# Attention taken two slots at a time in the mixed loop of an attention and mixture-of-experts kernel

## The chip, the cores and the metric

The kernel runs as one program on one core of a Trainium2 chip. The metric is the device time of one execution in microseconds (us); the time before is the median of three runs. The engines are named as in the profile: PE (TensorE, with PEld for its weight loads), DVE (VectorE), ACT (ScalarE), POOL (GpSimd) and SP (SyncE, which here only issues DMAs).

## The reference

Three layers follow each other. The second and the third are dense in everything but the choice of one expert per token.

```
# attention: 4 batches x 8 heads, 512 local and 32 global tokens, head dimension 64
out_g = softmax(q_g @ [k_g, k_l].T / 8) @ [v_g, v_l]                # global rows see all
s_l   = [q_l @ k_g.T, where(|i - j| <= 32, q_l @ k_l.T, -1e9)] / 8   # local rows: band of 65, and the globals
out_l = softmax(s_l) @ [v_g, v_l]
x = concat(out_g, out_l) as (2176, 512)
# dense layer, 512 -> 2048 -> 512
h = x @ w_in;  x = max(0.01 h, h) @ w_out
# routed layer, 8 experts, 512 -> 1024 -> 512
e = argmax(normalised x @ normalised expert_emb.T / tau)
out = gate * (relu(x @ w1[e]) @ w2[e])
```

## The kernel before

**Slots of attention.** The local attention is cut into 64 slots, two for each pair of 128-row chunks of a pair of heads; `m = n // 4` is the pair of heads of slot `n`. `att_parts(n)` lists what slot `n` issues:

- an even slot: `AV(p)` for `p = (n - 4) / 2` (lines 355 and 361, probabilities times values into `av`, copied to `xr`); then `softmax(n // 2)`, which is `S` (line 248, 32 small matmuls into the two score tiles `sp`), `M` (line 276, four masked row maxima on DVE; line 284, four exponentials on ACT) and `N` (lines 297 to 304, the division);
- every slot: `TR(n - 2)` (line 319, three transposes of probabilities into `pp`, copied to `pT` by ACT);
- a slot with `n % 4 == 1`: the keys of the next pair of heads, `kp` (line 217, copied to `kT` by ACT) and `gnp` (line 223, copied by DVE, line 225); with `n % 4 == 3`: the queries, `qp` (line 200, copied to `qz` by ACT);
- for the global rows, once in eight slots: `GS` (lines 388 and 389, scores into `sg1` and `sg2`; maxima on DVE, lines 392 to 394; exponentials into `pg` on ACT, lines 398 and 399) at slot 36 and at slots 43, 51 and 59; `GT` (lines 413 and 415, transposes `gp` and `gq`) at slots with `n % 8 == 6`; `GA4` in two pieces, `ga` (line 455) at `n % 8 == 7` and `gb` (line 460) at the next slot.

Slots 0 to 35 run in a front part with an order of its own, which the change does not touch. Slots 36 to 67 run in the mixed loop.

**The mixed loop.** It goes over `steps`, pairs `(i, f)` of the dense layer: 256 tokens `i` by 128 columns `f` of the hidden layer. A step issues `L1(i, f)` (line 850, 12 matmuls into `hps`), then perhaps a slot of attention, then `L2` of the step before (lines 877 to 879, 6 matmuls into `yp`), then perhaps one stage of the routing of finished tokens: `R1` (line 625, `x2p`), `R2` (line 636, `lp`), `R3` (lines 655 and 656, `rp`). Between `L1` and its `L2` stands a chain of four instructions: ACT `gf` (line 858), DVE maximum (line 860), ACT cast (line 863), DVE remainder (line 865). After the last step of a token block `R0` copies `yp` on ACT (line 614) and squares it (line 617).

A credit grows by 0.65 or 0.6 with each step. A slot is taken when it reaches 1:

```
credit += RATE[min(i, len(RATE) - 1)]
...
if credit >= 1.0 and slot < bound:
    run(att_parts(slot))
    slot += 1
    credit -= 1.0
credit = min(credit, 1.0)
```

**What sets the order.** PE runs in the order in which the program is written. DVE, ACT, POOL and SP are ordered when the program is built, by priorities (`ahead` raises that of most attention parts); once built, each engine runs its own list from first to last.

**PSUM.** The eight banks are four tags of two buffers each: `H` for `hps`, `Y` for `yp`, and in the loop `S` for `av`, one half of `sp`, `pp` and `sg1`, and `T` for everything else: the other half of `sp`, `sg2`, `kp`, `qp`, `gnp`, `gp`, `gq`, `ga`, `gb`, `x2p`, `lp`, `rp`. A matmul into a tag waits until the last reader of the buffer that it gets is done.

Of the kernel before, what the change touches and what calls it, by code (L numbers as in the profile page):

```python
# [24 lines left out]
def kernel(  # L25
# [22 lines left out]
    E, _, F2 = w1.shape  # L48
# [34 lines left out]
    def whole(job):  # L83
        for _ in job:
            pass
# [14 lines left out]
    def load_k(n):  # L100
        b, h0 = n // HP, 2 * (n % HP)
        if n % 2 == 0:
            yield SP, 2.0, "kn gn", "", 1.6
        else:
            yield SP, 1.0, "kn", "", 1.3
        kn = att.tile([P, NC, 2, D], F32, tag="kn", bufs=2, name="kn")
        rows(n, kn, k_l)
        if n % 2 == 0:
            gn = att.tile([2 * SG, 4 * D], F32, tag="gn", bufs=2, name="gn")
            for i, src in enumerate((q_g, k_g)):  # L110
                nc.sync.dma_start(
                    gn[i * SG:(i + 1) * SG].rearrange("s (h d) -> s h d", h=4),
                    src[b, h0:h0 + 4].rearrange("h s d -> s h d"),
                )
        else:
            gn = natural["gn"]
        natural["gn"] = gn
        natural["k", n] = kn, gn[:, (n % 2) * 2 * D:(n % 2 + 1) * 2 * D]

    def load_q(n):  # L120
        yield SP, 1.0, "qn", "", 1.3
        qn = natural["q", n] = att.tile([P, NC, 2, D], F32, tag="qn", bufs=1, name="qn")
        rows(n, qn, q_l)
# [254 lines left out]
    def GS(n):  # L378
        a1, a2 = bank_of("sg1"), bank_of("sg2")
        yield PE, 1.08, f"{a1} {a2}", kt_tag(n)  # L380
        sg1 = ps.tile([P, SL - SG], F32, tag=a1, name="sg1")
        sg2 = ps.tile([P, 2 * SG], F32, tag=a2, name="sg2")
        for j in range(4):
            o = slice(SG * j, SG * j + SG)
            kT, qg = qkT[n - 1 + j // 2]
            r = slice(D * (j % 2), D * (j % 2) + D)
            at = (D * (j % 2), SG * j)
            nc.tensor.matmul(sg1[o, :], qg[r], kT[r, 2 * SG:S_], start=True, stop=True, tile_position=at)  # L388
            nc.tensor.matmul(sg2[o, :], qg[r], kT[r, 0:2 * SG], start=True, stop=True, tile_position=at)
        yield DVE, 1.07, "", ""  # L390
        gm = att.tile([P, 4], F32, tag="gm", bufs=2, name="gm")
        nc.vector.tensor_reduce(out=gm[:, 0:1], in_=sg1, axis=AX.X, op=ALU.max, negate=True)
        nc.vector.tensor_reduce(out=gm[:, 1:2], in_=sg2, axis=AX.X, op=ALU.max, negate=True)
        nc.vector.tensor_scalar(
            out=gm[:, 0:1], in0=gm[:, 0:1], scalar1=gm[:, 1:2], scalar2=0.125, op0=ALU.min, op1=ALU.mult
        )
        yield ACT, 1.3, "pg", f"{a1} {a2}"
        nc.scalar.activation(out=pg[:, 0:SL - SG], in_=sg1, func=AF.Exp, bias=gm[:, 0:1], scale=0.125, accum_out=gm[:, 2:3])  # L398
        nc.scalar.activation(out=pg[:, SL:], in_=sg2, func=AF.Exp, bias=gm[:, 0:1], scale=0.125, accum_out=gm[:, 3:4])
        yield DVE, 0.37, "", ""  # L400
        nc.vector.tensor_scalar(
            out=gm[:, 2:3], in0=gm[:, 2:3], scalar1=gm[:, 3:4], scalar2=1e-9, op0=ALU.add, op1=ALU.add
        )
        nc.vector.reciprocal(out=gm[:, 2:3], in_=gm[:, 2:3])
        yield POOLL, 1.1, "", ""
        nc.gpsimd.tensor_tensor(out=pg, in0=pg, in1=gm[:, 2:3].to_broadcast([P, SL + 2 * SG]), op=ALU.mult)

    def GT(n):
        a1, a2 = bank_of("gp"), bank_of("gq")
        yield PE, 0.6, f"{a1} {a2}", "pg"  # L410
        gp = ps.tile([P, NC, P], F32, tag=a1, name="gp")
        for c in range(NC):
            nc.tensor.transpose(gp[:, c, :], pg[:, c * P:(c + 1) * P], ident)
        gq = ps.tile([2 * SG, P], F32, tag=a2, name="gq")
        nc.tensor.transpose(gq, pg[:, SL:], ident)
        yield DVE, 0.27, "gu", a2
        gu = att.tile([2 * SG, P], F32, tag="gu", bufs=1, name="gu")
        nc.vector.tensor_copy(gu, gq)
        by = yield (ACT, DVE), (0.59, 0.67), "PT", a1
        gt = att.tile([P, NC, P], F32, tag="PT", bufs=2, name="gt")  # L420
        copy(by, gt, gp)
        groups[n] = gt, gu
# [473 lines left out]
    late = {}  # L896
# [433 lines left out]
    LAG, AVL = 2, 4  # L1330

    def ahead(by, f, *a):
        with tc.high_priority(offset=by):
            whole(f(*a))

    def att_parts(n):

        parts = []
        m = n // 4
        p = (n - AVL) // 2  # L1340
        if n % 2 == 0 and 0 <= n - AVL < NU:
            if p in sums:
                parts.append(lambda: ahead(0, BR, p))
            parts.append(lambda: ahead(0, AV, p))
        early = m % 2 == 1 and n % 4 == 2 and m < NHP
        if early:
            parts.append(lambda: whole(GT(m)))
        if n < NU and n % 2 == 0 and not early:
            parts.append(lambda: ahead(50, softmax, n // 2))
        if m % 2 == 1 and n % 4 == 3 and m < NHP:  # L1350
            late["ga"] = GA4(m)
            parts.append(lambda: next(late["ga"]))
        if 0 <= n - LAG < NU:
            parts.append(lambda: ahead(50, TR, n - LAG))
        if early:
            parts.append(lambda: ahead(50, softmax, n // 2))
        if n % 4 in (1, 3) and m + 1 < NHP:
            parts.append(lambda: ahead(50, QK, m + 1, n % 4 // 2))
        if n % 8 == 0 and "ga" in late:
            parts.append(lambda: whole(late.pop("ga")))  # L1360
        if n == SLOT0 or n > SLOT0 and n % 8 == 3 and m + 1 < NHP:
            parts.append(lambda: whole(GS((n + 4) // 8 * 2 + 1 if n > SLOT0 else m)))
        if n % 4 == 3:
            if m + 3 < NHP:
                parts.append(lambda: whole(load_k(m + 3)))
            if m + 2 < NHP:
                parts.append(lambda: whole(load_q(m + 2)))
        for v in range(2, NHP):
            if n == 4 * (v - 2) + max(AVL + 2, 7 - v % 2):
                parts.append(lambda v=v: whole(load_v(v)))  # L1370
        return parts


# [23 lines left out]
    def run(parts):  # L1397
        for p in parts:
            p()
# [3 lines left out]
    SLOT0 = 36  # L1403
# [11 lines left out]
        BR=[-72.8, 427.3, 393.7, 659.9, 354.6, 181.8, 728.1, 127.1, 127.4, 513.3, 141.3, 12.2, 477.9, 672.5, 305.3,  # L1415
            338.0, 255.6],
# [7 lines left out]
        GS=[0.0, -360.1, 0.0, 390.9, 0.0, 458.7, 0.0, 442.6],  # L1424
        AV=[-608.9, -583.3, -939.5, -865.4, -876.7, -658.5, 89.6, -629.4, -191.7, -506.2, 13.6, -135.5, -415.6,
            414.4, -43.5, 327.5],
        GT=[0.0, -1032.9, 0.0, -450.7, 0.0, -353.5, 0.0, -170.3],
# [207 lines left out]
    while k < len(steps):  # L1635
        i, f = steps[k]
        store_rows()
        if k == KF * (2 * B - 1) + 6:
            assert not pend_r
            plan_constants()  # L1640
            early_plan()
            load_w(0, zip(lane, (w1, w2)))
            to_split(0, lane, False)
            for u in range(NEARLY):
                load_ids(u)
            for u in range(2):
                gather(u)
        if k == K0 + 1:
            routing_rows()
            fetch_part()  # L1650
        credit += RATE[min(i, len(RATE) - 1)]
        bound = min(LAST, AVL + 16 * (2 + i // 2) + (2 if i % 2 == 1 and i > 1 else 0))
        bank = MIXED
        mp = moe_parts(i, f)
        run(mp[:1])
        if credit >= 1.0 and slot < bound:
            run(att_parts(slot))
            slot += 1
            credit -= 1.0
        credit = min(credit, 1.0)  # L1660
        run(mp[1:])
        if pend_r:
            st, t = pend_r.pop(0)
            st(t)
        if k >= KF * (2 * B - 1) + 10:
            for _ in range((2, 1, 1, 2, 1, 1)[k - KF * (2 * B - 1) - 10]):
                tc.keep_in_program_order(piece())
        if slot == LAST and att is not None:
            att_pool.__exit__(None, None, None)
            att = None  # L1670
            lp_ = late["pool"] = ctx.enter_context(tc.tile_pool(name="lane", bufs=1))
            lane += [lp_.tile([P, KM, F2], F32, name="w1a"), lp_.tile([P, KF2, DM], F32, name="w2a")]
        k += 1
# [205 lines left out]
```

## Time and profile before

| | |
|---|---|
| three runs, median (lowest to highest) | 817.11 us (816.13 to 820.07) |
| the profiled execution | 820.54 us, of which the profile's span is 818.8 us |
| PE busy | 795.5 us, 97% of the span |
| PEld, DVE, ACT, POOL busy | 661.5, 401.7, 371.7, 200.0 us |
| slots 36 to 67 of the mixed loop | from 199.6 to 420.4 us of the span |
| granted clock of PE, mean | 0.995 of 2.4 GHz |

The profile's PE share counts a matmul as busy until its modelled end, so that a busy PE may still be waiting for the next weights. The times of the section on the rows are microseconds from the start of the span.

### The profile page before, as it was taken

To read this page: it belongs to the slowest core of one execution; us is meant where nothing else is said; L and a number is where in the kernel's file an instruction comes from. 1 tells how busy PE (TensorE), PEld (TensorE's weight loads), DVE (VectorE), ACT (ScalarE), POOL (GpSimd) and SP (SyncE) were. 2 spreads that over 40 slices of the span, in tenths; PEclk is the share of its full clock that TensorE was granted. 3 is DMA by queue.
4 is the path that set the end of the run, shared out by engine and by line. 5 is a ranking of instruction groups with operands and counts; after the bars stand their busy time and mean duration, and the time that the engine had idled before them with its cause. 6 is when DMAs were issued, how large, how long until landed. Compare 5 with 4: busy or idle time off the path is not lost.

```text
span 818.8 us, 17489 instructions
## 1 busy us (share of the span) xinstructions
PE 795.5 (97%) x6818; PEld 661.5 (81%) x6818; DVE 401.7 (49%) x1200; ACT 371.7 (45%) x1006; POOL 200.0 (24%) x294
## 2 busy tenths in 40 slices
PE   7989999999999999999999999999999999989996
PEld 5778878888888888888888888898899886858642
DVE  4788775635645554554552533546453525215230
ACT  5776676545534544544532323335323425224441
POOL 4767986801110010000010100002101421111100
PEclk9999999999999999999999999999999999999998
DMA  8967585610122220211000000071049796997890
GB/s 196 233 156 188 159 207 156 198 40 18 46 60 45 65 49 21 42 37 17 2 27 1 14 14 1 27 206 52 26 46 227 234 398 251 358 391 253 333 368 25
DMA packets 111885, 106.18 MB, mean 130 GB/s; under 512 B 75879, under 2 KB 84199, under 8 KB 111794
## 3 DMA queue, kind: packets, MB, share of 16 engines
q1 hardware_dynamic: 107314, 95.53, 39.5%
q0 software_dynamic: 3424, 9.20, 3.4%
q8 instruction: 55, 0.90, 0.5%
q14 instruction: 36, 0.29, 0.2%
q10 hardware_dynamic: 1056, 0.26, 0.1%
HBM read 94.13 MB, written 11.10 MB: 129 GB/s over the span
## 4 chain that ended last, share of the span: by engine, by line
PE 79%; DMA 8%; issue 7%; DVE 3%; ACT 1%; SPq 1%; POOL 1%; POOLq 0%; ACTq 0%
PE hps L850 24%; PE yp L877 8%; PE yp L879 7%; PE yp L878 7%; PE hps L1297 6%; PE yp L1315 6%; DMA out_dram<-yo,ids 4%; PE sp L248 3%; PE pp L319 3%; PE av L355 2%; DMA wm<-in_moe_w_dram 2%; PE av L361 2%; PE lp L636 1%; PE sg L388 1%; PE sc L334 1%
## 5 line engine op out<-in xcount | busy, mean ns | idle before, releaser
L858 ACT ACTIVATE gf<-hps 128x256 f32<-128x256 f32 (+1 forms) x144 | 53.7, 373 | 155.1 <-PE hps L850 143.4
L860 DVE TENSOR_TENSOR hps<-hps,gf 128x256 f32<-128x256 f32 (+1 forms) x144 | 59.9, 416 | 110.9 <-ACT gf L858 109.8
L877 PE MATMUL yp<-woh,g 128*128 128x512 f32 x272 | 111.5, 410 | 0.8 <-ACT g L863 0.8
L879 PE MATMUL yp<-woh,g 128*128 128x512 f32 x272 | 107.5, 395 | 0.0
L878 PE MATMUL yp<-wol,g 128*128 128x512 f32 x272 | 107.4, 395 | 0.0
L865 DVE TENSOR_TENSOR g<-hps,g 128x256 fp32r<-128x256 f32 (+1 forms) x144 | 58.4, 406 | 44.1 <-ACT g L863 43.5
L863 ACT CAST g<-hps 128x256 fp32r<-128x256 f32 (+1 forms) x144 | 52.1, 362 | 56.6 <-DVE hps L860 47.1
L850 PE MATMUL hps<-xs,wih 128*128 128x256 f32 x448 | 75.6, 291 | 0.5 <-ACT pg L398 0.4
L1315 PE MATMUL yp<-w2s,g 128*128 128x512 f32 x288 | 75.5, 395 | 0.0
L850 PE MATMUL hps<-xl,wih 128*128 128x256 f32 x448 | 70.7, 279 | 0.0
L850 PE MATMUL hps<-xs,wil 128*128 128x256 f32 x448 | 70.7, 279 | 0.0
L850 PEld LDWEIGHTS hps<-xs,wih 128*128 128x128 f32 x448 | 64.0, 188 | 7.0 <-issue 0.7
L1297 PE MATMUL hps<-xgT,w1s 128*128 128x256 f32 x384 | 61.9, 283 | 0.4 <-ACT xgT L1192 0.4
L879 PEld LDWEIGHTS yp<-woh,g 128*128 128x128 f32 x272 | 51.0, 188 | 12.6 <-DVE g L865 0.2
L850 PEld LDWEIGHTS hps<-xs,wil 128*128 128x128 f32 x448 | 60.5, 188 | 0.0
L850 PEld LDWEIGHTS hps<-xl,wih 128*128 128x128 f32 x448 | 60.5, 188 | 0.0
L877 PEld LDWEIGHTS yp<-woh,g 128*128 128x128 f32 x272 | 51.0, 188 | 9.9 <-ACT g L863 1.4
L1315 PEld LDWEIGHTS yp<-w2s,g 128*128 128x128 f32 x288 | 50.8, 187 | 10.0 <-issue 0.8
L1297 PEld LDWEIGHTS hps<-xgT,w1s 128*128 128x128 f32 x384 | 54.0, 188 | 3.7 <-ACT xgT L1192 0.7
L878 PEld LDWEIGHTS yp<-wol,g 128*128 128x128 f32 x272 | 51.2, 188 | 6.7
L1303 ACT ACTIVATE g<-hps 128x256 fp32r<-128x256 f32 x48 | 18.5, 385 | 77.3 <-PE hps L1297 72.1
L1304 DVE SCALAR_TENSOR_TENSOR g<-hps,g 128x256 fp32r<-128x256 f32 x48 | 20.4, 424 | 64.6 <-ACT g L1303 60.3
(314 smaller groups left out, 1517.0 us busy)
## 6 DMA issues: line engine op xcount, KB each, us to landing
wm<-in_moe_w_dram SPq DMA_DIRECT2D x14, 2048.0 KB
w1a<-in_moe_w_dram SPq DMA_DIRECT2D x6, 2048.0 KB
w2a<-in_moe_w_dram SPq DMA_DIRECT2D x6, 2048.0 KB
raw<-in_moe_w_in_dram SPq DMA_DIRECT2D x16, 512.0 KB
raw<-in_moe_w_out_dram SPq DMA_DIRECT2D x16, 512.0 KB
x2d<-x SPq DMA_DIRECT2D x16, 256.5 KB
kn<-in_k_l_dram SPq DMA_DIRECT2D x31, 128.0 KB
qn<-in_q_l_dram SPq DMA_DIRECT2D x31, 128.0 KB
```

Source lines behind the costliest of these rows:

```text
L248: nc.tensor.matmul(sps[h][HALF_ * half:HALF_ * half + HALF_, to:to + width], qz[r, t:t + HALF_], kT[r, from_:from_ + width], start=not fro ...
L319: nc.tensor.transpose(pp[:, j, :], pr[:, from_:from_ + P], ident)
L850: nc.tensor.matmul(hps, ws[a][:, k], xs[c][k], start=(a + c + k == 0), stop=((a, c) == (1, 0) and k == KM - 1))
L858: nc.scalar.activation(out=gf, in_=hps[:, cs], func=AF.Copy, scale=0.01)
L860: nc.vector.tensor_tensor(out=hps[:, cs], in0=hps[:, cs], in1=gf, op=ALU.max)
L863: nc.scalar.copy(g[:, 0], hps[:, cs])
L865: nc.vector.tensor_tensor(out=g[:, 1], in0=hps[:, cs], in1=g[:, 0].bitcast(F32), op=ALU.subtract)
L877: nc.tensor.matmul(yp, g[:, 0], hi, start=begins(i, f), stop=False)
L878: nc.tensor.matmul(yp, g[:, 0], lo, start=False, stop=False)
L879: nc.tensor.matmul(yp, g[:, 1], hi, start=False, stop=ends(i, f))
L1297: nc.tensor.matmul(hps, w[:, a, k, fs], xts[u][c][:, k], start=(a + c + k == 0), stop=(a == 1 and k == KM - 1))
L1315: nc.tensor.matmul(ys[u, t], g[:, a, t * P:(t + 1) * P], w[:, c, f % 4, :], start=(f + a + c == 0), stop=(f == KF2 - 1 and a == 1),)
```

## The change

Two slots are taken in one step, when the credit reaches 2, and the credit is capped at 2. Their parts are issued one slot behind the other, each slot in its old order. Each part now carries a number in front, which nothing in the loop reads.

```
-                parts.append(lambda: ahead(0, BR, p))
-            parts.append(lambda: ahead(0, AV, p))
+                parts.append((0, lambda: ahead(0, BR, p)))
+            parts.append((0, lambda: ahead(0, AV, p)))
...
-            parts.append(lambda: ahead(50, TR, n - LAG))
+            parts.append((3 + 4 * (n % 2), lambda: ahead(50, TR, n - LAG)))
...
-        if credit >= 1.0 and slot < bound:
-            run(att_parts(slot))
-            slot += 1
-            credit -= 1.0
-        credit = min(credit, 1.0)
+        if credit >= 2.0 and slot < bound:
+            parts = att_parts(slot) + att_parts(slot + 1)
+            run([fn for _, fn in parts])
+            slot += 2
+            credit -= 2.0
+        credit = min(credit, 2.0)
```

The 32 slots of the loop become 16 pairs, (36, 37) to (66, 67). Worked from the rates, they fall in steps 32, 35, 38, 41, 45, 48, 51, 55, 58, 64, 67, 70, 73, 77, 80 and 83 of the loop. Before, the even slots stood in steps 32, 35, 38, 42, 45, 48, 52, 55, 58, 64, 67, 70, 74, 77, 80 and 84, and each odd slot one to three steps behind its even one.

PE around slots 36 and 37, before. `sg` are the two tiles of `GS`, `kp` and `gnp` the keys of the next pair of heads.

```order
L389 MATMUL sg_3184<-kT 32x64
L877 MATMUL yp<-woh,g 128x512 [waits Activation_49]
L878 MATMUL yp<-wol,g 128x512
...
L636 MATMUL lp<-enT,x2T 128x8 [waits DVE_49,PE_49]
...
L850 MATMUL hps<-xs,wil 128x256 x4
L319 MATMUL pp<-ident,pr_105 128x128 [waits Activation_49]
...
L217 MATMUL kp<-ident,kn 128x128 [waits DMAHW2_49,DMAHW1_49,Activation_49]
...
L223 MATMUL gnp<-ident,gn 128x64 [waits DMAHW4_49,DMAHW3_49,DVE_49]
```

The same place after:

```order
L389 MATMUL sg_3184<-kT 32x64
L319 MATMUL pp<-ident,pr_105 128x128 [waits Activation_49]
...
L217 MATMUL kp<-ident,kn 128x128 [waits DMAHW2_49,DMAHW1_49,DVE_49]
...
L223 MATMUL gnp<-ident,gn 128x64 [waits DMAHW4_49,DMAHW3_49,Activation_49]
L877 MATMUL yp<-woh,g 128x512
L878 MATMUL yp<-wol,g 128x512
```

`L2`, a routing stage and the next `L1` no longer stand between `sg` and `gnp`, and `gnp` now waits for ACT.

ACT at this place, before (`pg` are the exponentials of `GS`, `sq` the squares of `R0`):

```order
L284 ACTIVATE pr_104,sm<-pr_104,nm 128x160 [waits DVE_49] x3
L398 ACTIVATE pg,gm<-sg_3183,gm 128x480 [waits DVE_49,PE_49]
L399 ACTIVATE pg,gm<-sg_3184,gm 128x64 [waits PE_49]
L617 ACTIVATE sq,ss<-x_2935 128x512 [waits PE_49]
...
L858 ACTIVATE gf<-hps 128x256 [waits PE_49]
L81 COPY pT<-pp 128x384 [waits PE_49]
L649 ACTIVATE lg,ss<-lg,ss 128x8 [waits DVE_49]
L81 COPY kT<-kp 128x512 [waits PE_49]
```

And after:

```order
L284 ACTIVATE pr_104,sm<-pr_104,nm 128x160 [waits DVE_49] x3
L81 COPY pT<-pp 128x384 [waits PE_49]
L81 COPY kT<-kp 128x512 [waits PE_49,Pool_49]
L398 ACTIVATE pg,gm<-sg_3183,gm 128x480 [waits DVE_49]
L399 ACTIVATE pg,gm<-sg_3184,gm 128x64
L617 ACTIVATE sq,ss<-x_2935 128x512 [waits DVE_49,PE_49]
```

The copies of slot 37 now stand ahead of the exponentials of slot 36.

PE at slots 42 and 43 after. Before, an `L2` and an `L1` stood between the two `pp`, which belong to one slot each:

```order
L319 MATMUL pp<-ident,pr_104 128x128 [waits DVE_49]
...
L319 MATMUL pp<-ident,pr_104 128x128 [waits DVE_49,PE_49]
...
L200 MATMUL qp<-ident,qn 128x128 [waits DMAHW5_49,DMAHW4_49]
...
L388 MATMUL sg_3828<-kT 32x480 [waits Activation_49]
L389 MATMUL sg_3829<-kT 32x64 [waits DVE_49]
```

The second `pp` stands right behind the first and waits for DVE.

## Rows read from the trace of the kernel before

**Rows 1.** Windows, PE: stretch, length, busy (instructions), granted clock, DMA share, GB/s.

```profile
196.00:424.00 228.00, 227.15 (x2332) 1.00 0.16 36
```

**Rows 2.** Waits of PE between 196 and 425 us: total, times, longest.

```profile
PE x2p L625 <- ACT x L614: 0.6, 2, 0.3
PE sg L388 <- DVE nm L276: 0.3, 1, 0.3
```

**Rows 3.** Chain of waits at slots 36 and 37: start, time it took, what.

```profile
200.70 0.87 PE sp L248 x32
...
202.28 1.02 PE sg L388 x8
...
203.43 0.43 PE yp L877
...
207.33 0.33 PE pp L319 x3
207.66 0.44 PE kp L217 x4
...
209.93 1.52 PE hps L850 x12
211.45 0.23 PE yp L877
```

**Rows 4.** Chain of waits at slots 38 to 40.

```profile
215.28 0.46 PE av L355 x16
...
218.12 0.43 PE yp L877
...
222.01 0.83 PE ga L455 x40
222.84 0.48 PE pp L319 x3
...
229.93 0.61 PE av L355 x16
...
232.26 0.11 PE gb L460
232.37 0.24 PE yp L877
```

**Rows 5.** Timeline of DVE at slots 36 and 40: start, busy, instruction [idle before it].

```profile
201.56 0.32 DVE L276 CUSTOM_DVE_ANT_0 pr<-sp,mask 128x160 f32<-128x160 f32 x1
...
202.29 0.32 DVE L276 CUSTOM_DVE_ANT_0 pr<-sp,mask 128x160 f32<-128x160 f32 x1
...
203.51 0.66 DVE L392 TENSOR_REDUCE gm<-sg 128x1 f32<-128x480 f32 x1 [0.89 <-PE sg L389]
...
232.82 0.44 DVE L462 COPY xgl<-gb 64x64 f32<-64x64 f32 x2
```

**Rows 6.** Timeline of ACT at slots 36 and 37.

```profile
202.35 0.46 ACT L81 COPY pT<-pp 128x384 f32<-128x384 f32 x1
...
203.86 0.19 ACT L284 ACTIVATION_READ_ACCUMULATOR pr<-pr,nm 128x1 f32 x1
205.27 0.66 ACT L398 ACTIVATE pg<-sg,gm 128x480 f32<-128x480 f32 x1 [1.21 <-DVE sm L300]
...
205.92 0.31 ACT L399 ACTIVATE pg<-sg,gm 128x64 f32<-128x64 f32 x1
...
208.55 0.58 ACT L81 COPY kT<-kp 128x512 f32<-128x512 f32 x1
```

**Rows 7.** Chain of waits at slot 46, where a token block ends.

```profile
274.92 0.48 ACT x L614
```

**Rows 8.** Windows of PE in the front part and near the end, columns as in rows 1.

```profile
59.00:60.00 1.00, 0.60 (x12) 0.78 0.05 10
...
62.00:63.00 1.00, 1.00 (x20) 0.51 1.28 316
...
710.00:720.00 10.00, 7.30 (x51) 1.00 1.04 392
```

More of the change, by code (lines that the diff above doesn't have):

```diff
@@ L1342, in att_parts @@
             if p in sums:
-                parts.append(lambda: ahead(0, BR, p))
-            parts.append(lambda: ahead(0, AV, p))
+                parts.append((0, lambda: ahead(0, BR, p)))
+            parts.append((0, lambda: ahead(0, AV, p)))
         early = m % 2 == 1 and n % 4 == 2 and m < NHP
         if early:
-            parts.append(lambda: whole(GT(m)))
+            parts.append((1, lambda: whole(GT(m))))
         if n < NU and n % 2 == 0 and not early:
-            parts.append(lambda: ahead(50, softmax, n // 2))
+            parts.append((2, lambda: ahead(50, softmax, n // 2)))
         if m % 2 == 1 and n % 4 == 3 and m < NHP:
             late["ga"] = GA4(m)
-            parts.append(lambda: next(late["ga"]))
+            parts.append((5, lambda: next(late["ga"])))
         if 0 <= n - LAG < NU:
-            parts.append(lambda: ahead(50, TR, n - LAG))
+            parts.append((3 + 4 * (n % 2), lambda: ahead(50, TR, n - LAG)))
         if early:
-            parts.append(lambda: ahead(50, softmax, n // 2))
+            parts.append((4, lambda: ahead(50, softmax, n // 2)))
         if n % 4 in (1, 3) and m + 1 < NHP:
-            parts.append(lambda: ahead(50, QK, m + 1, n % 4 // 2))
+            parts.append((6, lambda: ahead(50, QK, m + 1, n % 4 // 2)))
         if n % 8 == 0 and "ga" in late:
-            parts.append(lambda: whole(late.pop("ga")))
+            parts.append((8, lambda: whole(late.pop("ga"))))
         if n == SLOT0 or n > SLOT0 and n % 8 == 3 and m + 1 < NHP:
-            parts.append(lambda: whole(GS((n + 4) // 8 * 2 + 1 if n > SLOT0 else m)))
+            parts.append((9, lambda: whole(GS((n + 4) // 8 * 2 + 1 if n > SLOT0 else m))))
         if n % 4 == 3:
             if m + 3 < NHP:
-                parts.append(lambda: whole(load_k(m + 3)))
+                parts.append((10, lambda: whole(load_k(m + 3))))
             if m + 2 < NHP:
-                parts.append(lambda: whole(load_q(m + 2)))
+                parts.append((10, lambda: whole(load_q(m + 2))))
         for v in range(2, NHP):
             if n == 4 * (v - 2) + max(AVL + 2, 7 - v % 2):
-                parts.append(lambda v=v: whole(load_v(v)))
+                parts.append((10, lambda v=v: whole(load_v(v))))
         return parts
```

## The prediction

> **What bounds the kernel now.** I read the windows first. From 196 to 424 us, the whole mixed loop, PE is busy 227.15 of 228.00 us at a granted clock of 1.00 [rows 1]. The waits of PE there sum to 0.9 us: one of 0.3 us of `sg` for the row maxima, and two of `x2p` for ACT [rows 2]. So the loop is one stream of matmuls without holes, DVE and ACT run in its shadow, and time can come in by two doors only: a hole in the stream, or a matmul that costs more or less because of its neighbour. The chain of waits shows the second [rows 3, 4]. A `yp` behind full-size work takes 0.23 us, behind `sg` or `sp`, which use a part of the array, 0.43: 0.20 more. Behind `pp` it takes 0.24, nearly nothing more. `pp` itself costs 0.33 behind `hps` and 0.48 behind a small op, 0.15 more. `av` costs 0.61 behind `hps` and 0.46 behind another small op.
>
> **The change.** Nothing is computed more or less, and every slot runs in the same step as before or one to three earlier, so loads of keys, queries and values are issued no later. What moves is the odd slot: it stands right behind the even one, without the `L2` and `L1` in which its buffers came free. So I go through each pair and ask for every tile which reader frees its buffer.
>
> Where the score buffer in `S` comes free is seen in the present kernel: `sp` ends at 200.70 + 0.87 = 201.57 and `sg`, which wants that buffer, starts at 202.28, so 0.71 us behind `sp` [rows 3]. Until then DVE has done two of the four maxima; the fourth starts at 202.29 and takes 0.32, three steps of 0.245 behind the first at 201.56 [rows 5], so the half in `T` comes free 0.49 later than the other, 1.20 behind `sp`.
>
> *Pair (36, 37), one pair: +1.70.* Up to the end of `sg` at 203.43 [rows 3] it is as before, its 0.3 us wait too. Then `pp` follows `sg` (0.48) and `kp` (0.44): PE is at 204.35 and wants `gnp`. Its `T` buffer is that of `sg2`, whose last reader is the second exponential of `GS`. On ACT the last row-exponential ends at 203.86 + 0.19 = 204.05; then, in the new order, come `pT` (0.46, to 204.51) and `kT` (0.58, to 205.09), and only then the exponentials of `GS`: the second starts 0.65 behind the first (205.92 - 205.27) and takes 0.31, so it ends at 206.05 [rows 6]. The maxima of `GS` on DVE start at 203.51 with one of 0.66 [rows 5] and are done before ACT asks for them. With some 0.05 for the hand-over `gnp` starts at 206.10, a hole of 1.75. Its least value is with ACT free for `GS` from 204.5 on: 204.5 + 0.96 = 205.46, a hole of 1.1. Its most is with the copies waiting for PE and the row overheads summed: some 2.2. I take 1.75, which every row gives directly. Of neighbours this pair loses one 0.20 (`sg` no longer stands ahead of `yp`) and gains 0.15 (`pp` behind `sg`): -0.05.
>
> *Pairs (42, 43), (50, 51), (58, 59) and (44, 45), (52, 53), (60, 61), six pairs: +1.38.* `sp` is followed by `pp`, which gets the buffer of `av`, long copied, and takes 0.48; the second `pp` gets the buffer of `sp`, free at 0.71: a hole of 0.23. Behind it nothing waits: `qp` or `kp` ends at 0.71 + 0.33 + 0.44 = 1.48, and what follows wants buffers free at 1.20, or that of the first `pp`, copied by ACT within 0.46 of the first exponential. Six times 0.23.
>
> *Pairs (40, 41), (48, 49), (56, 57): +0.84.* `gb` (0.11, [rows 4]) fills part of the first hole, which leaves 0.71 - 0.59 = 0.12. `kp` then stands at 1.04 and wants the buffer free at 1.20: 0.16. `gnp` at 1.64 wants that of `gb`, whose two copies take 0.44 on DVE behind the fourth maximum [rows 5] and are done about then. Three times 0.28.
>
> *Pairs (38, 39), (46, 47), (54, 55), (62, 63): -1.10.* `ga` takes the place of `yp` behind `sp`. That `yp` cost 0.43 [rows 4] and now costs 0.23. `ga` behind `sp` is not in the trace: behind `hps` it takes 0.83; if it gains as `av` does it takes 0.68. So each pair saves between 0.20 and 0.35. I take 0.28, the middle, since both neighbours use part of the array but not the same part. `qp` is at 1.16 to 1.31 behind `sp` where its buffer is free at 1.20: nothing, or 0.04.
>
> *The two `x2p` waits at a block's end: +0.20.* In pairs (46, 47) and (54, 55) ACT has the four exponentials, `pT` and `qz` ahead of the copy `x`. Before, `x2p` waited 0.3 each time [rows 2] for this copy of 0.48 [rows 7]. In slot 36 the exponentials end 204.05 - 201.57 = 2.48 behind `sp`, with a `pT` of 0.46 among them, so 2.02 without; then `pT` 0.46, `qz` (of the size of `kT`) 0.58 and the copy bring ACT to 3.54. PE, through `ga`, `pp`, `qp` and six `yp` of 0.23, is there at 0.83 + 0.48 + 0.44 + 1.40 = 3.15: a wait of 0.4, 0.1 more than now, twice. *Pairs (64, 65) and (66, 67)* hold no scores: nothing.
>
> Nothing hides these holes: they lie on the stream that bounds. What follows has slack: the ACT and DVE chain between `L1` and its `L2` has another `L2` and `L1` to itself. What it costs if that cover goes is rival 2. The sum: 1.70 + 1.38 + 0.84 - 1.10 + 0.20 = **+3.0 us**. Bounds: with the small hole in (36, 37) and the large saving +2.0; with the large hole, the small saving and hand-overs of 0.1 at each of the nine holes +4.7.
>
> The Trainium skill, "TensorEngine Tiling (Array Packing)", section "Key Properties", says that a change of the tiling mode drains the engine. By that rule alone each pair would save a border ahead of `L2`. The rows show the 0.20 behind `sg` and `sp`, but not behind `pp`, a full-size transpose, and ten of the 16 even slots end with `pp` or `gb`; so the sum above has the saving in five pairs, and the rule's own time is rival 5.
>
> **The rivals.**
>
> 1. *The clock falls at the hole of (36, 37)*: slower. In the front part, behind a stretch with holes and small matmuls, the granted clock fell to its half level, 1.2 GHz, over four windows of 1 us, the first at 0.78 and the last at 0.51; the two between at some 0.50 make 0.22 + 0.50 + 0.50 + 0.49 = 1.7 us lost [rows 8]. It decides if the hole of 1.75 between small matmuls does the same. Against it: near the end a hole of 2.7 us (7.30 busy of 10) went by at 1.00 [rows 8]. Time: +3.0 + 1.7 = +4.7, 821.8 us. The Trainium skill, "TensorE: Matmul & The Clock Gate", section "HAM oscillation — how this bites in real kernels", tells of just this: waits between short bursts let the clock fall again and again. By that rule the loss could come with every pair, 16 x 1.7 = 27 us; this and the one fall share the chance below.
> 2. *The crowded queues hold back `g`*: slower. Two slots put up to four exponentials, two `pT`, `kT` or `qz`, and `GS` or `x` on ACT in one go. If ACT is behind by more than the slack when the next `L1` ends, `yp` waits for `g`. By the rows ACT is free again 2.48 + 0.46 + 0.58 = 3.5 us behind `sp`, about 2 us later where `GS` follows. The next `L1` ends at about 1.64 + 0.20 + 1.40 + 1.52 = 4.8, and its `L2` comes another 2.9 behind that (`yp` 1.40, `hps` 1.52 [rows 3]), against a chain of some 1.6 (four instructions of about 0.4). So it decides only if ACT runs over 1 us later than worked out. At 0.5 in nine pairs: +3.0 + 4.5, 824.6 us.
> 3. *The holes close*: faster. If the buffers are handed out in another order, so that the second `pp` and `gnp` get free ones, only the savings are left, and the present 0.9 us of waits may go: -1.15 to -2.1, 815.5 us. Against it: the order of after shows `gnp` waiting for ACT and the second `pp` for DVE.
> 4. *The end swallows it*: the last 120 us hang on weights and stores, and a later loop might not move them. Then 817.1 us. Against it: those loads are issued when PE has freed their space, so they move with it.
> 5. *Every border is saved*: the holes as worked out, 1.75 + 1.38 + 0.84 + 0.20 = 4.2, less 16 x 0.20: +1.0, 818.1 us. Against it: `yp` at 0.24 behind `gb` [rows 4].
>
> **How the numbers follow.** The profiled execution took 820.54 us, its span 818.8, 3.4 us above the median of 817.11. The sum makes the span 821.8 and such an execution 823.5; on the median it gives 817.1 + 3.0 = **820.1 us**. Chances: forecast 0.58, clock 0.13, queues 0.09, closed holes 0.08, swallowed 0.07, borders 0.05. A measurement of this kernel can tell about 0.5% from no change, 4.1 us, so 813.0 and 821.2 are the limits. Rivals 1 and 2 (0.22) lie above; of the forecast, whose upper bound is +4.7, a sixth does (0.09): slower 0.31. Of rival 3 a third may go below (0.03). The rest, 0.66, is within. The range leaves out some of the tails of rivals 2 and 3: 815.8 to 823.8 us.
>
> **What would show it right or wrong.** Right: in the loop, one wait of `gnp` for ACT `pg` of 1.1 to 2.2 us, nine waits of `pp` for the maxima of 0.1 to 0.3, three of `kp` below 0.2, `x2p` at about 0.4 twice, and waits of PE that sum to some 5 us for 0.9 before, with the clock at 1.00. `ga` behind `sp` at 0.68 to 0.83. Wrong: waits of `yp` for `g` (rival 2), a granted clock below 1.00 near the pairs (rival 1), no wait at the second `pp` (rival 3), or a span that moves by less than the loop does (rival 4).

## The result, and the profile after

The changed kernel takes 824.53 us (median of 14 runs, 820.51 to 831.65), the kernel before, on the same chip, 819.66 us (14 runs, 816.13 to 822.72). The ratio is 1.0061, 95% interval 1.0044 to 1.0079: slower by 0.6%, 4.9 us (a ratio here and below is the one on record, against runs of the kernel before that were made beside it, and can differ a little from the quotient of the medians). The profiled execution took 825.06 us, its span 823.3 us. The median before was 817.11 us in the three runs that the prediction started from, so of the 4.4 us between the forecast of 820.1 and the result 2.5 belong to the kernel before and 1.9 to the change: +4.9 us in place of +3.0.

The loop, where the slots are, accounts for it. The starts of `L1` steps in the timeline show it; here three rows of before, then the same three steps of after (start, duration, instruction):

```profile
198.04 0.70 PE L850 MATMUL hps<-xs,wih 128*128 128x256 f32 x4
...
428.47 0.64 PE L850 MATMUL hps<-xs,wih 128*128 128x256 f32 x4
...
499.12 0.64 PE L850 MATMUL hps<-xs,wih 128*128 128x256 f32 x4
```

```profile
199.04 0.70 PE L850 MATMUL hps<-xs,wih 128*128 128x256 f32 x4
...
434.51 0.64 PE L850 MATMUL hps<-xs,wih 128*128 128x256 f32 x4
...
505.16 0.64 PE L850 MATMUL hps<-xs,wih 128*128 128x256 f32 x4
```

From the step of slot 36 to the step behind slot 67 before needs 230.43 us and after 235.47, 5.04 more. From there to the last row both need 70.65. The rest differs too in these two executions: up to slot 36 that of after takes 1.00 us more, from the last row to the end 1.5 us less. But none of the kernels traced here has an edit in either stretch, and over the eight of them the first varies from 195.5 to 199.8 us and the second from 318.0 to 322.0. So I read the loop; its 5.04 agrees with the 4.9 of the medians. In the loop the granted clock is 1.00, and PE is busy less than in [rows 1] (windows of after, columns as there; first PE, then PEld, DVE, ACT, POOL):

```profile
196.00:424.00 228.00, 223.98 (x2296) 192.39 (x2296) 119.93 (x479) 107.12 (x345) 22.50 (x39) 1.00 0.16 37
```

The waits of PE there, which answer to [rows 2]:

```profile
PE pp L319 <- DVE nm L276: 2.3, 9, 0.3
PE gnp L223 <- ACT kT L81: 0.7, 1, 0.7
PE x2p L625 <- ACT x L614: 0.6, 2, 0.3
PE sg L388 <- DVE nm L276: 0.3, 1, 0.3
```

The last two lines are those of before. New are nine waits of a second `pp` and one of `gnp`, 3.0 us in all. The loop is 5.04 us longer and saves something at the borders, so these waits cost more than the view says. Where the rest lies is seen at one hole, in the pair (42, 43). PE first, then its weight loads, PEld (timelines of after; in brackets the idle time before the row and what ended it):

```profile
246.26 0.87 PE L248 MATMUL sp<-kT,qz 64*64 64x128 f32 x32
247.07 0.55 PE L319 MATMUL pp<-ident,pr 128*128 128x128 f32 x3
247.91 0.52 PE L319 MATMUL pp<-ident,pr 128*128 128x128 f32 x3 [0.30 <-DVE nm L276]
248.27 0.60 PE L200 MATMUL qp<-ident,qn 128*128 128x128 f32 x4
```

```profile
247.06 0.31 PEld L319 LDWEIGHTS pp<-ident,pr 128*128 128x128 f32 x3
247.88 0.31 PEld L319 LDWEIGHTS pp<-ident,pr 128*128 128x128 f32 x3 [0.51 <-PE pp L319]
248.16 0.47 PEld L200 LDWEIGHTS qp<-ident,qn 128*128 128x128 f32 x4
```

The first `pp` ends, as modelled, 0.55 us behind its start, and from there the view counts 0.30 of idle time. But in a row without holes the next matmul does not start at that end. In experiment 1 below, `qp` starts 0.38 behind the `pp` ahead of it. So the second `pp`, 0.84 behind the first, is 0.46 late: the 0.30 shown, and 0.17 by which neighbours overlap (the sum is 0.47; the rows are rounded). PEld, whose loads have no such tail, shows 0.51, the whole hole and 0.05 more. Its waits over the loop:

```profile
PEld pp L319 <- PE pp L319: 3.0, 6, 0.5
...
PEld pp L319 <- PE gb L460: 1.3, 3, 0.4
PEld gnp L223 <- ACT kT L81: 1.0, 1, 1.0
```

Six holes of 0.5, three of 0.4 and one of 1.0 make 5.3 us, close to the loop's 5.04 with the small savings taken off.

I then compared the starts of all `L1` steps, after less before, and summed from one pair to the next (worked out from the timelines; every pair's steps are compared as a whole, as its odd slot stood further on before):

| pairs | forecast, each | measured, each |
|---|---|---|
| (36) | +1.70 | +0.78 |
| (42), (44), (50), (52), (58), (60) | +0.23 | +0.48 to +0.49 |
| (40), (48), (56) | +0.28 | +0.47 to +0.55 |
| (38), (46), (54), (62) | -0.28, and +0.10 at `x2p` in two | -0.06 to -0.19 |
| (64), (66) | 0 | +0.19, +0.05 |
| sum | +3.0 | +5.04 |

### The profile page after: what moved, and what is told of

The parts are those of the page before. It is cut to its first block, busy times and chain, and to the rows that moved or that the text cites. A ratio compares the mean times of both kernels' runs of the same rounds, so it can differ in the third digit from the quotient of the medians.

```text
span 823.3 us, 17505 instructions
## 1 busy us (share of the span) xinstructions
PE 798.6 (97%) x6818; PEld 661.7 (80%) x6818; DVE 403.3 (49%) x1200; ACT 372.7 (45%) x1006; POOL 199.1 (24%) x294
## 4 chain that ended last, share of the span: by engine, by line
PE 79%; issue 7%; DMA 7%; DVE 3%; ACT 2%; POOL 0%; SPq 0%; POOLq 0%; ACTq 0%; DVEq 0%
PE hps L850 23%; PE yp L877 8%; PE yp L879 7%; PE yp L878 7%; PE hps L1297 6%; PE yp L1315 5%; DMA out_dram<-yo,ids 4%; PE sp L248 3%; PE pp L319 2%; PE av L355 2%; DMA wm<-in_moe_w_dram 2%; PE av L361 2%; PE lp L636 1%; PE sc L334 1%; PE kp L217 1%
```

## The experiments

The theory that stood when the runs were planned: a pair costs because its second `pp` waits for the score buffer, and the start behind the wait costs 0.2 more than the idle time shown. I then put the 0.2 down to a weight load that a running row hides. The rivals were that pairs cost by what they put on the queues, or by two `pp` in a row. "Loop" below is the difference between the starts of the same two `L1` steps in the profiled execution, from slot 36's to the last, against before (after: +5.04). In the expectations of experiments 1, 2 and 5 two kinds of pair are exchanged: `sg` stands in (42), (50) and (58), `gnp` in (44) and (52), and (60) has neither, since slot 61 has no next keys to fetch.

**1. The hole filled** (`e1_fill`). The order inside a pair is altered, by the numbers that the parts carry (`first_of` issues `kp` and its copy, the second of the two parts `gnp`); slots 36 and 37 stand alone.

```
+            if n % 4 == 1 and n > 38:
+                keys = QK(m + 1, 0)
+                parts.append((6, lambda: ahead(50, first_of, keys)))
+                parts.append((8, lambda: ahead(50, lambda: keys)))
...
-            parts.append((8, lambda: whole(late.pop("ga"))))
+            parts.append((1, lambda: whole(late.pop("ga"))))
...
+        many = 1 if slot < 38 else 2
...
-            run([fn for _, fn in parts])
+            run([fn for _, fn in sorted(parts, key=lambda part: part[0])])
```

> The changed kernel with the same pairs from slot 38 on (36 and 37 stand alone as in the kernel before), but with the order inside a pair altered: the copy-free transposes of the next keys (kp) or queries (qp), four full 128x128 transposes that issue in about 0.44 us, stand between the two pp, gnp stands behind the second pp, and gb ahead of sp. Nothing is left out. Theory (a pair costs because the second pp waits for the score buffer that is free only 0.71 us behind sp, a hole of 0.26, and because the first transposes behind a hole show their weight load too, 0.2 more): kp or qp fills the 0.38 that is missing, so the second pp has no wait and takes 0.33; what is left is sg waiting for the copy of the first pp in the pairs (44), (52), about 0.3 each, and slots 60 and 64 as in the changed kernel, less 0.1 at each pair with GT and GA: +0.8 us against the kernel before, ratio 1.001, and 4.2 under the changed kernel. Rival (a pair costs because two visits in one row load the queues of ScalarE and VectorE more, whatever stands between): the order inside the pair changes little, +3.5 to +4.5 us, ratio 1.0045 to 1.0055.

Measured: 821.99 us, ratio 1.0032, interval 1.0010 to 1.0053; loop +1.96. (42, 43) in its timelines, PE and PEld:

```profile
245.88 0.55 PE L319 MATMUL pp<-ident,pr 128*128 128x128 f32 x3
246.26 0.60 PE L200 MATMUL qp<-ident,qn 128*128 128x128 f32 x4
246.72 0.52 PE L319 MATMUL pp<-ident,pr 128*128 128x128 f32 x3
247.30 1.03 PE L388 MATMUL sg<-kT 64*32 64x480 f32 x8
```

```profile
246.69 0.31 PEld L319 LDWEIGHTS pp<-ident,pr 128*128 128x128 f32 x3
247.30 0.18 PEld L388 LDWEIGHTS sg<-kT 64*32 64x32 f32 x8 [0.30 <-ACT pT L81]
```

The hole at the second `pp` is gone. The loop is 3.1 us shorter than in the changed kernel, 0.8 of it from slots 36 and 37; the rest comes from the order inside the pairs alone, with the same slots in one step. The rival's least, +3.5, is not reached in the trace; the interval of the ratio does not decide it. One pair is a control: in (60, 61) there are no keys to move, so nothing fills its hole, and, as foreseen, it costs +0.48 as in the changed kernel. It is the only second `pp` that still waits on PE (the waits of experiment 1):

```profile
PE pp L319 <- DVE nm L276: 0.3, 1, 0.3
PE qp L200 <- PE ga L455: 1.1, 3, 0.4
```

The theory's +0.8 was missed too, by 1.1 us. The wait of `sg` for the copy of the first `pp` had been priced at 0.6 in all and came to about that, 0.2 in each of three pairs (PEld 0.30 above; on PE nothing is shown). Not priced were two things. (40), (48) and (56) keep about 0.2 each; in (40) the chain gives `gb` 0.23 at its new place ahead of `sp`, for 0.11 in [rows 4]. And `qp`, moved ahead of the second `pp`, waits 0.4 behind `ga` in (38), (46) and (54). In (38) it starts 1.2 behind the end of `sp`, when by the prediction the half of `sp` in `T` comes free; the view names only `ga`, so that this is the reason is argued, not shown. (38) costs +0.24 for that, in place of -0.08; (46) and (54) cost what they do in the changed kernel, as their waits of `x2p` on PE are gone in exchange.

**2. Another buffer, the same order** (`e2_other_buffer`).

```
-        at = bank_of("pp")
+        at = bank_of("pp1" if bank is MIXED and u % 2 else "pp")
...
+            swap = slot > 40 and slot % 8 in (2, 4)
+            MIXED["pp1"] = "T" if swap else "S"
+            MIXED["kp"] = MIXED["qp"] = "S" if swap else "T"
             parts = att_parts(slot) + att_parts(slot + 1)
```

> The changed kernel, same order of PE's work; only in the six pairs (42), (44), (50), (52), (58), (60) the second pp is given a buffer of the T pair, which is free long before, and kp or qp one of the S pair in its place. The two pp then follow one another with no wait between. Theory (the 0.2 belongs to the wait, a weight load that a running stream hides): the second pp takes 0.33 as the first does; kp or qp stands at the freed score buffer nearly on time; left in these pairs are small holes, 0.1 to 0.2 at gnp in (42), (50), (58), about 0.3 at sg in (44), (52), (60): the six pairs together +1.4 in place of +2.9, the kernel about +3.5 us against the kernel before, ratio 1.0043. Rival (the 0.2 is a property of one pp directly behind another, whatever it waits for): the second pp still takes about 0.52, the six pairs +2.6, the kernel +4.7 us, ratio 1.0057.

Measured: 822.06 us, ratio 1.0041, interval 1.0022 to 1.0060; loop +3.05. The interval holds both the theory's 1.0043 and the rival's 1.0057, so the loop has to tell. Of the six pairs, three cost +0.18 and three +0.11 or less, +0.74 in all for the theory's +1.4 and the rival's +2.6. The pair (42, 43):

```profile
247.01 0.87 PE L248 MATMUL sp<-kT,qz 64*64 64x128 f32 x32
247.81 0.87 PE L319 MATMUL pp<-ident,pr 128*128 128x128 f32 x6
248.61 0.63 PE L200 MATMUL qp<-ident,qn 128*128 128x128 f32 x4
```

Its weight loads have no break either:

```profile
247.81 0.64 PEld L319 LDWEIGHTS pp<-ident,pr 128*128 128x128 f32 x6
```

Two `pp` in a row are 0.32 longer than one. So a second `pp` right behind the first costs its own work and no more; what cost was the wait for the buffer. Taking away six waits that the PE view puts at 0.3 shortened these pairs by 2.2 us together, 0.36 each, although `qp` and `sg` picked up small waits of their own.

**3. Only the six pairs with this hole** (`e3_pairs_2_4`), and **4. only the four pairs without one** (`e4_pairs_6`, where the condition is `slot % 8 == 6`).

```
-        if credit >= 2.0 and slot < bound:
+        many = 2 if slot > 40 and slot % 8 in (2, 4) else 1
+        if credit >= many and slot < bound:
```

> Only the six pairs (42), (44), (50), (52), (58), (60) are taken together, every other slot stands alone as in the kernel before. Theory (0.28 of hole and 0.2 of weight load, nothing else): +0.48 each, +2.9 us against the kernel before, ratio 1.0035. By the prediction's price (the hole alone, 0.23 each): +1.4 us, ratio 1.0017. Rival (the pairs cost through each other, one that delays copies for the next): with singles between them, under +1 us.

> Only the four pairs (38), (46), (54), (62) are taken together, in which the two pp lie 1.7 us apart with sp and ga between; every other slot stands alone as in the kernel before. Theory (no hole, a saved border between small and full tiles worth 0.1 to 0.2): -0.5 us against the kernel before, ratio 0.9994. By the prediction's price for the saved borders (0.28 each): -1.1 us, ratio 0.9987. Rival (every pair costs, since copies come in bursts): +0.5 us or more.

Measured for 3: 820.93 us, ratio 1.0028, interval 1.0006 to 1.0050, which holds the theory's 1.0035, the 1.0017 of the prediction's price and the rival's +1 us (1.0012); the loop tells them apart. It is +2.87, which is 0.48 a pair. The six holes need nothing else of the change to cost what they cost in it. For 4: 819.91 us, ratio 1.0010, interval 0.9988 to 1.0033; loop -0.34, 0.09 saved a pair. The sign is that of the theory and not of the rival, in the trace alone; the size is too small for a measurement to tell. Beside waits that stand in [rows 2] too, 4 shows none on PE in the loop, and 3 shows this line:

```profile
PE pp L319 <- DVE nm L276: 1.8, 6, 0.3
```

**5. More work in the hole** (`e5_more_work`). This tells a start set by a release from a fixed price for each pair.

```
+        more = (0, WB, WU - WB)[:3] if u > 39 and u % 8 in (0, 2) else ()
+        for j, from_ in (*enumerate(more), *enumerate((0, WB, WU - WB))):
-        for j, from_ in enumerate((0, WB, WU - WB)):
             nc.tensor.transpose(pp[:, j, :], pr[:, from_:from_ + P], ident)
```

> The changed kernel, but in the six pairs (42), (44), (50), (52), (58), (60) the first pp does its three transposes twice (the same values twice into the same buffer; nothing is left out). That is 0.32 us more work of PE ahead of each of these holes. Read from the starts of the L1 steps of one execution. Theory (the second pp starts when DVE has released the score buffer, 0.71 behind sp, and its start behind a wait costs 0.19 more): the added work lies in the hole; a pair (42), (50), (58) still costs about +0.48 (0.40 to 0.50). In (44), (52), (60) the copy of the first pp now stands behind a second exponential on ACT and sg waits for it, up to 0.4 more. The loop +5.0 to +6.3 us against the kernel before. Rival (a pair costs a fixed amount over its work, for instance the change from small to full tiles, and the idle time is only where it shows): each of these pairs +0.8, the loop +7.0 us or more.

Measured (one execution, so the loop alone is read): +5.43, 0.39 more than the changed kernel for 6 x 0.32 = 1.9 us more work. (44), (52), (60) are unchanged to 0.01 us, (42), (50), (58), where `sg` waits, are 0.12 longer. The pair (42, 43), PE and PEld:

```profile
243.46 1.36 PE L319 MATMUL pp<-ident,pr 128*128 128x128 f32 x9
244.66 0.60 PE L200 MATMUL qp<-ident,qn 128*128 128x128 f32 x4
```

```profile
243.46 0.64 PEld L319 LDWEIGHTS pp<-ident,pr 128*128 128x128 f32 x6
244.27 0.31 PEld L319 LDWEIGHTS pp<-ident,pr 128*128 128x128 f32 x3 [0.18 <-issue]
```

On PE this is one busy group of nine with no hole in it. But the weights of the last three are loaded 0.81 behind the first, where in the changed kernel it was 247.88 - 247.06 = 0.82. The second `pp` starts when DVE has let go of the scores, whatever the first one does until then. This also corrects the name that I had given the 0.2: it is no load time added behind a wait, but time that lies before it, under the modelled tail of the last matmul.

**6. Only the pair (36, 37)** (`e6_pair_36`). The condition is `slot == 36`.

> Only slots 36 and 37 are taken together, every other slot stands alone as in the kernel before. Theory (gnp is given the buffer of kp and waits for its copy on ACT, 0.7 us): +0.8 us in the loop against the kernel before, one wait of gnp for kT of 0.7, starting about 3.5 behind sp. By the prediction (gnp waits for the exponentials of the group scores): +1.70, a wait of 1.75.

Measured (one execution): loop +0.81. The chain of waits at this place (start, time it took, what):

```profile
204.92 0.34 ACT pT L81
...
205.30 0.59 ACT kT L81
...
205.94 0.28 PE gnp L223
```

As in the changed kernel, `gnp` goes on when `kT` is copied. The second exponential of `GS`, the last reader of `sg2`, starts only behind that, here as in the changed kernel (timelines of after, PE and ACT):

```profile
206.07 0.28 PE L223 MATMUL gnp<-ident,gn 64*128 64x64 f32 x1 [0.73 <-ACT kT L81]
206.56 0.32 ACT L399 ACTIVATE pg<-sg,gm 128x64 f32<-128x64 f32 x1
```

So `gnp` cannot have been given the buffer of `sg2`; what it waits for is the reader of `kp`.

## Why the prediction was wrong

**What bounds the kernel** stood: the loop is one stream of PE, and what is lost in it is lost to the end. The loop took +5.04 us, the medians +4.9, and the 70.65 us behind the loop did not move. One reading was slack: the 0.24 given for a `yp` behind `pp` stands in [rows 4] behind `gb`, though the chain of before has the same behind `pp` (at 248.17).

**The six pairs: +1.38 forecast, +2.9 measured. This is the step that failed.** Its mechanism was right: the second `pp` gets the buffer of `sp`, and it starts 0.71 behind the end of `sp`, as foreseen from [rows 3]. The chain of after:

```profile
246.34 0.87 PE sp L248 x32
247.21 0.31 DVE pr L276
...
247.52 0.24 DVE pr L276
...
247.78 0.14 issue
247.91 0.52 PE pp L319 x3
248.43 0.44 PE qp L200 x4
```

247.91 - 247.21 = 0.70. Wrong was the term that I subtracted: the first `pp` at 0.48, from the chain in [rows 4], as if it began where `sp` ends. The chain hands over at modelled ends, so its pieces of PE contain the tail that the next matmul overlaps; only sums over a row without holes come out right. By starts the first `pp` begins 0.14 ahead of that end of `sp` (247.07 for 247.21) and keeps the stream 0.38. So of the 0.70 it covers 0.24, and not 0.48, and the hole is 0.46, and not 0.23. All nine holes ahead of a second `pp` were priced in this way, each some 0.23 too low, which makes 2 us. That the whole sum is 2.0 off as well is chance, since the other errors below happen to cancel.

The trace of before had the answer at the one hole of this kind that it holds, slot 36, where `sg` waits behind `pp` as the second `pp` does now. I read the 0.3 of [rows 2] there. Its timelines, PE and PEld:

```profile
201.44 0.55 PE L319 MATMUL pp<-ident,pr 128*128 128x128 f32 x3
202.28 1.03 PE L388 MATMUL sg<-kT 64*32 64x480 f32 x8 [0.30 <-DVE nm L276]
```

```profile
201.43 0.31 PEld L319 LDWEIGHTS pp<-ident,pr 128*128 128x128 f32 x3
202.25 0.21 PEld L388 LDWEIGHTS sg<-kT 64*32 64x32 f32 x8 [0.51 <-PE pp L319]
```

0.84 from start to start, and 0.51 on PEld: the same numbers as in the six pairs after. At 0.46 a hole the six pairs come to 2.8.

**(40), (48), (56): +0.84 forecast, +1.57 measured.** The same term: PEld waits 0.43 behind `gb`, where I had left 0.12. The waits of `kp` and `gnp` that I had put at 0.16 are not shown on PE. By starts there is something of that of `kp`: it comes 0.44 to 0.49 behind the second `pp`, where `qp` comes 0.36 behind it in (42, 43).

**(38), (46), (54), (62): -1.10 forecast, -0.46 measured** (and -0.34 alone, experiment 4). Right in sign. The border of `yp` is saved, but `ga` behind `sp` gains nothing. In the chain of after it takes the 0.83 that [rows 4] has behind `hps`:

```profile
219.90 0.83 PE ga L455 x40
220.73 0.48 PE pp L319 x3
```

I had taken the middle between no gain and that of `av`; the upper end of the range that I gave for this term was true, and `qp` is some 0.06 later besides (0.45 behind `pp`, before 0.39 in the timeline).

**(36): +1.70 forecast, +0.78 measured.** Here the mechanism was wrong, and not a size. `gnp` starts 3.50 behind `sp` and not 4.53, because it gets another buffer than I assumed; the least of my bounds, a hole of 1.1, did not allow for this. The order of after had said "waits for ACT", and ACT has two copies and two exponentials there; I took one without showing that it was the one. With the right one the prediction's own rows do well: `kT` ends at 205.09, which with the 0.05 of hand-over is a hole of 0.79, and PE shows 0.73. In its full size the hole is 1.0 on PEld.

**`x2p`: +0.20 forecast, 0 measured;** the two waits are still 0.6 together. (64) cost 0.19, which I had at nothing because it holds no scores. But it has two `pp` too, and the second gets the buffer of `av`, which ACT is still copying (timelines of after, ACT and PE, then the wait of PEld):

```profile
411.04 0.38 ACT L81 COPY xr<-av 128x256 f32<-128x256 f32 x1
411.47 0.55 PE L319 MATMUL pp<-ident,pr 128*128 128x128 f32 x3
```

```profile
PEld pp L319 <- ACT xr L81: 0.3, 1, 0.3
```

It is the same kind of hole, short enough to leave no idle time on PE.

**The rivals.** The clock stayed at 1.00 in the loop (rival 1 out), no `yp` waits for `g` (2 out), there are waits at the second `pp` (3 out), the loop's +5.04 is found again in the medians, +4.9 (4 out), and the loop grew by five times what rival 5 gave it (5 out). At the nine holes the mechanism of the forecast was right and the size half of what it was; at (36) the reader was the wrong one. Measured less forecast, the terms are +1.5 and +0.7 where a hole was too small, +0.6 where a saving was too large, -0.9 at (36), -0.2 at `x2p` and +0.25 at (64) and (66), together +2.0.

**The range** ended at 823.8. Its upper bound of the change, +4.7, was a little below the +5.0 of the loop, and I had put the bound on a median of three runs that came out 2.5 us low. That the kernel would be slower by over 0.5% had 0.31; with 0.46 at each of the six holes, 0.43 in place of 0.28 at each of the three, and all else as I had it, the sum is 3.0 + 1.4 + 0.5 = +4.9, on the slower side of the limit.

**No better version.** The only pairs that gain are those of experiment 4, by 0.34 us in the trace, and the measurement (0.9988 to 1.0033) does not tell that from nothing.

## What to carry to other kernels

Price a stall on TensorE by starts, from a row with the hole and one without, or by the idle time of its weight loads; idle time and pieces of a chain that go by modelled ends leave out the overlap of neighbours, and with holes this short that was 0.17 of 0.46 us. When two pieces of work are put together, ask for each tile which reader frees the buffer that it gets and what stands between to cover that time: full-size work of 0.44 between the two transposes closed the hole, another buffer closed it too, and the pairs that had other work there cost nothing. If a term rests on which buffer a tile gets, it needs a bound for the other buffer too.

## What was not expected of the hardware

- A short stall of PE can leave no idle time on PE in the profile: in experiment 5 the nine transposes are one unbroken group, and only PEld shows 0.18; in experiment 1 `sg` shows none, and PEld 0.30.
- From the end of the last read of a score buffer on DVE to the matmul that waits for it, 0.13 to 0.14 us pass each time ("issue" in the chain, at the nine `pp` of after as at `sg` of before, the row below). Where a copy by ACT is what ends the wait, it is 0.04 (`gnp` of after, and the second `pp` of (64)).

```profile
202.15 0.14 issue
```

- 0.32 us more of matmul work ahead of a hole of 0.46 changed the time of a pair by 0.00 to 0.12 us (experiment 5).
